# Threshold attention and a bilinear FFN on one core: another order inside the first ten slots

## The chip, the cores and the metric

The kernel runs on one core of one Trainium2 chip, as one launch. The time is device microseconds (us) of that core. The core has a matrix engine (TensorE, "PE" in the profile, with its weight loads as "PEld"), a vector engine (VectorE, "DVE"), an activation engine (ScalarE, "ACT"), a general engine (GpSimd, "POOL") and a queue that issues the transfers (SyncE, "SP"). Each works through its own list of instructions in the order in which the program wrote it, and waits on semaphores of the others.

## The reference

```python
# q, k, v: (8, 8, 576, 64) float32, tau = 0.02; w_a, w_b: (512, 1536), w_out: (1536, 512), float64
scores = 1/sqrt(64) * q @ k^T
thresh = max(scores, -1) - tau
scores = where(scores >= thresh, scores, -1e9)
scores = scores - max(scores, -1)
attn   = exp(scores); attn = attn / (sum(attn, -1) + 1e-9)
x      = (attn @ v) with the heads beside each other        # (4608, 512)
out    = ((x @ w_a) * (x @ w_b)) @ w_out                    # (4608, 512) float32
```

The weights of the FFN arrive as float64 and are made float32 on the chip, by operations on their two 32-bit halves.

## The kernel before

**Units and slots.** Attention is cut into 160 units. A unit is 128 rows of the queries of two heads (a pair), or the last 64 rows of both. The loop at line 756 runs over slots: slot g computes the scores of unit g, its exponentials, mask and sums, and carries units g-1 and g-2 (in the first ten slots) further. After the loop the rest of the FFN follows. The order in which the program writes the instructions is kept on every engine (`keep_order`), so where a call stands in the loop is where its instructions stand in each engine's list.

**What one of the first slots does**, for the unit of slot g, in the order of before:

- `scores` (line 314): 16 records of products on TensorE, two row maxima on VectorE (L332), two biases (L334) and one threshold (L336) on GpSimd.
- `weighted_unit` (line 499), in slots 2 to 9, for unit g-2: `product` (L479, TensorE, product with v), then `join`: a copy out of PSUM on ScalarE (L468) and an addition of the other half on VectorE (L469); then `exchange`, two copies on GpSimd (L489).
- `convert_sign` and `convert_shift` (L238, L246, VectorE) and `convert_add` (L251, GpSimd) for the weight pieces that slot g-1 began.
- `load_weights`: transfers of the next weight pieces on SP's queue, when a staging buffer is free, which the sign operation frees.
- `weigh` (line 353): two exponentials on ScalarE (L364), then two operations on VectorE that mask and sum (L367).
- `turn_pe` (line 396), in slots 1 to 8, for unit g-1: 16 records of products that turn and scale the weights (L406, TensorE), two copies on ScalarE (L408), 4 records more (L412), one copy on VectorE (L414).
- `convert_first` (L225, L226, ScalarE) and `convert_clamp` (L232, GpSimd) of one piece, then `reciprocal` (L376, L380), `diagonals` (L393, ScalarE; from unit 8 on `normalise`, L386), then the slot's other pieces. Slots 0 to 3 begin two pieces, slots 4 to 9 three.
- `advance`: steps of the FFN on TensorE. The amount is counted in columns: a slot has a `pace`, and `advance` runs steps until the columns owed are paid. A step of the first block has 128 columns (8 records of L578 in the trace). In slots 0 to 8 the whole pace, 0.04 x 36864 + 576 = 2051 columns, comes at the end of the slot, and 640 columns are taken off for `product`. If there is no block to work on, what is owed is dropped. The first block exists from slot 5 on, when the product of unit 3 is joined.

One step in eight ends a group of products: after the eighth with `wa_sb` ScalarE copies the result out (L584), after the eighth with `wb_sb` VectorE multiplies (L586). Until then the group holds its PSUM buffer.

**PSUM.** All results of TensorE go through one pool of four buffers (`banks`, two banks each). A unit's two score buffers are held from the products to the mask operations, which read them again.

**Slots from 10 on** differ: the turning is done by VectorE transposes and transfers, and the FFN's columns come in four portions over the slot.

Of the kernel before, what the change touches and what calls it, by code (L numbers as in the profile page):

```python
# [10 lines left out]
FP32 = mybir.dt.float32  # L11
# [12 lines left out]
BY_PE = 8  # L24
# [8 lines left out]
PORTIONS = (0.3, 0.35, 0.15, 0.2)  # L33
RAWS = 4
BY_HEAD = 16


def keep_order(tc):
# [13 lines left out]
def kernel(  # L52
# [40 lines left out]
    P = 128  # L93
# [21 lines left out]
    def pool(name, bufs, **kw):  # L115
        return ctx.enter_context(tc.tile_pool(name=name, bufs=bufs, **kw))
# [4 lines left out]
    small = pool("small", 2)  # L121
# [3 lines left out]
    def banks(n, name):  # L125

        return psum.tile([P, 2, 512], FP32, tag="banks", name=name)[:, :, 0:n]
# [4 lines left out]
    loaded = {}  # L132
# [110 lines left out]
    def convert_shift(n):  # L243
        if n in stages:
            top = pieces[n][0].bitcast(U32)
            nc.vector.tensor_scalar(top, top, 3, None, op0=ALU.logical_shift_left)  # L246
# [43 lines left out]
    prepared, scored, weights, turned, tbufs = {}, {}, {}, {}, {}  # L290
# [23 lines left out]
    def scores(i, u):  # L314
# [3 lines left out]
        each = [(c, t, j) for c in range(2) for t in range(n) for j in range(2)]  # L318
        if units.index((i, u)) < BY_HEAD:
            each.sort(key=lambda x: x[2])  # L320
# [29 lines left out]
        t = t.rearrange("p n e -> p (n e)").rearrange("p (z n e) -> p z n e", z=4, e=Q)  # L350
        return [t[:, i]] if u == NT else [t[:, g % 2 * 2 + j] for j in range(2)]

    def weigh(i, u):

        sc, thr, bias, mx, biased = scored.pop((i, u))
        n = len(sc)
        sums = small.tile([P, 2], FP32, tag="sums", name="sums")
        ws = rooms_of(i, u)
        sb = [s.rearrange("p c (n e) -> p c n e", e=Q) for s in sc]
        wb = [w.rearrange("p (c n) e -> p c n e", c=2) for w in ws]  # L360
        for j in range(n):
            if not biased:
                nc.scalar.activation(bias[:, j:j + 1], mx[:, j:j + 1], AF.Copy, scale=e_nscale)
            nc.scalar.activation(wb[j], sb[j], AF.Exp, bias=bias[:, j:j + 1], scale=e_scale)  # L364
        for j in range(n):
            wv = wb[j]
            nc.vector.scalar_tensor_tensor(  # L367
                out=wv, in0=sb[j], scalar=thr[:, j:j + 1], in1=wv,
                op0=ALU.is_ge, op1=ALU.mult, accum_out=sums[:, j:j + 1])
        weights[i, u] = (ws, sums)  # L370
# [25 lines left out]
    def turn_pe(i, u):  # L396

        ws, dg = weights.pop((i, u))
        ws = [w.rearrange("p n e -> p (n e)") for w in ws]
        wT = work.tile([P, NSLOT, P], FP32, tag="wT", bufs=WT_BUFS, name="wT")  # L400
        turned[i, u, "pe"] = wT
        tp = banks(512, "tp").rearrange("p j (s q) -> p j s q", s=NT)
        for j, w in enumerate(ws):
            for s in range(NT):
                c = TAIL * j + s * P
                nc.tensor.matmul(tp[:, j, s, :], w[:, c:c + P], dg[:, j], start=True, stop=True)  # L406
        for j in range(2):
            nc.scalar.copy(wT[:, 5 * j:5 * j + NT], tp[:, j])  # L408
        tp = banks(P, "tp")[:, 0]
        for j, w in enumerate(ws):  # L410
            c = MAIN * (1 - j)
            nc.tensor.matmul(tp[TAIL * j:TAIL * (j + 1)], w[:, c:c + TAIL], dg[:, j],  # L412
                             start=True, stop=True)
        nc.vector.tensor_copy(wT[:, NT], tp)  # L414
# [56 lines left out]
    def product(wT, vm, n):  # L471

        pv = banks(n, "pv")
        for s in (NT, 0, 1, 2, 3):
            for r in range(2):
                rows = slice(r * D, (r + 1) * D)
                for j in ((r,) if s == NT else range(2)):
                    k0 = NT if s == NT else 5 * j + s
                    nc.tensor.matmul(pv[j * D:(j + 1) * D, r], vm[rows, k0], wT[rows, k0],  # L479
                                     start=(s == (NT if j == r else 0)), stop=(s == NT - 1))  # L480
        return pv

    def x_tile(name):
        return work.tile([P, HP, HALF], FP32, tag="xT", bufs=XT_BUFS, name=name)
# [11 lines left out]
                exchange(x, xs, hp, 0, HALF, nc.gpsimd)  # L496
            blocks.append(((x, xs), what))

    def weighted_unit(i, u):

        b, hp = pairs[i]
        pv = product(turned.pop((i, u, "pe")), loaded[i]["v"], P)
        if (b, 0) not in x_of:
            x_of[b, 0] = x_tile("xT")
            state["xs"] = x_tile("xS")
        join(x_of[b, 0][:, hp, u * P:(u + 1) * P], pv[:, 0], pv[:, 1])
        exchange(x_of[b, 0], state["xs"], hp, u * P, (u + 1) * P, nc.gpsimd)
        if hp == HP - 1:
            state["rows"] = u + 1
            if u == 0:  # L510
                blocks.append(((x_of[b, 0], state["xs"]), ("first", b, 0)))
# [181 lines left out]
    def cost():  # L693

        return BLOCK_COLS - (NF // 2 * CH if state["sums"] else 0)
# [34 lines left out]
    def backlog():  # L730
        return len(blocks) * cost() + (running["left"] if running["ffn"] is not None else 0)
# [3 lines left out]
    units = []  # L735
# [15 lines left out]
    n = 0  # L751
# [4 lines left out]
    for g in range(len(units) + PV_LAG):  # L756
        written = len(pending)
        here = g < len(units)
        converting = bool(early.get(g)) or bool(early.get(g - 1))
        if here:  # L760
            i, u = units[g]
            scores(i, u)
        turn_back()
        exchange_blocks()
        pace = (PACE if g > BY_PE else PACE_EARLY) * BLOCK_COLS
        if g > BY_PE:
            pace = min(pace, backlog() / (min([a for a in arrivals if a > g] + [len(units) + PV_LAG + 1]) - g))
        pace += (NSLOT + 1) // 2 * S / (NT + 1) + CATCH_UP * max(backlog() - BLOCK_COLS, 0)
        if 2 <= g < BY_PE + 2:
            weighted_unit(*units[g - 2])  # L770
            running["owed"] -= (NSLOT + 1) // 2 * P
        if g < 3:
            prep_copy(*prep_pe(g + 1, "q"))
        for n in early.get(g - 1, []):
            convert_sign(n)
        for n in early.get(g - 1, []):
            convert_shift(n)
        for n in early.get(g - 1, [])[-1:] + early.get(g - 1, [])[:-1]:
            convert_add(n)
        if g == 3:  # L780
            for c in range(0, NSUM - 2 * CW + 1, 2 * CW):
                extra.append(sums_u32[:, c:c + 2 * CW].rearrange("p (f w) -> p f w", w=2))
        load_weights(RAWS)
        if g > BY_PE and g <= len(units):
            turn_blocks(*units[g - 1])
        if g > BY_PE:
            advance(PORTIONS[0] * pace)
        if here:
            weigh(i, u)
        if 0 < g <= BY_PE:  # L790
            turn_pe(*units[g - 1])
        if g < 3:
            prep_copy(*prep_pe(g + 1, "k"))
        for p in range(HP, NPR):
            for name, d in (("q", 2), ("k", 1)):
                if g == first[p] - d:
                    prep(p, name)
        if g > BY_PE:
            advance(PORTIONS[1] * pace)
            n = g - PV_LAG  # L800
            if BY_PE <= n < len(units) and part(*units[n]):
                make_room()
                weighted(*part(*units[n]))
                running["owed"] -= (NSLOT + 1) // 2 * width(*part(*units[n]))
        for n in early.get(g, [])[:1]:
            convert_first(n)
            convert_clamp(n)
        if here:
            reciprocal(i, u, nc.scalar if converting else nc.vector)
        if here and g < BY_PE:  # L810
            diagonals(i, u)
        elif here:
            normalise(i, u)
        for n in early.get(g, [])[1:]:
            convert_first(n)
            convert_clamp(n)
        load_weights(RAWS)
        for p in range(HP, NPR):
            for name, d in (("q", 4), ("k", 3)):
                if g == first[p] - d:  # L820
                    load(p, name)
        for p in range(1, NPR):
            if g == first[p] - 1:
                load_v(p)
        store(written)
        advance((PORTIONS[2] if g > BY_PE else sum(PORTIONS[:3])) * pace)
        advance(PORTIONS[3] * pace)

        if not converting and not state["sums"]:
            state["slots"] = state.get("slots", 0) + 1  # L830
            for n in {1: (0,), 2: (1,), 3: (2,)}.get(state["slots"], ()):
                for z in range(2):
                    weight_sums(n, z)
            if state["slots"] >= 3 and state["through"]:
                for z in range(2):
                    weight_sums(3, z)
                state["sums"] = True
# [38 lines left out]
```

## Time and profile before

| | |
|---|---|
| median of 8 runs | 1480.96 us (1477.71 to 1483.95) |
| the profiled execution: its time, its span | 1478.24 us, 1476.4 us |
| busy, share of the span | PE 96%, PEld 82%, DVE 63%, ACT 45%, POOL 24% |
| mean granted TensorE clock | 0.994 |
| chain that ended last, by engine | PE 86%, DVE 5%, ACT 2%, the rest 7% |
| start of the scores of slots 2 to 10 | 25.86, 33.97, 39.48, 46.37, 56.47, 67.47, 76.53, 87.68, 101.0 us |

The time of an execution is its span and 1.84 us around it. The span runs from the first to the last instruction; all places in the trace are us from its start. Busy time of TensorE is modelled, since its products overlap. An engine's idle time matters only where it lies on the way to the end.

### The profile page before, as it was taken

The numbers are of one execution on the slowest core, as the hardware profiler recorded it, in microseconds if no ns is written. First come the engines' busy times: TensorE is split into PE (matmuls) and PEld (weight loads), VectorE is DVE, ScalarE is ACT, GpSimd is POOL, SyncE is SP. The second block draws the span as 40 slices with busy tenths as digits, with TensorE's granted clock in tenths as the row PEclk, the third lists the DMA queues.
The fourth block names the chain that finished last, engine by engine and source line by source line (L and its number), as shares of the span: only waits on it lengthen the run. The fifth ranks groups of instructions, "written<-read, shape, count | busy, mean of one in ns | idle before, by whom it ended". The sixth has DMA issues, their size and how long they took to land.

```text
span 1476.4 us, 57127 instructions
## 1 busy us (share of the span) xinstructions
PE 1419.5 (96%) x25344; PEld 1211.1 (82%) x25344; DVE 926.2 (63%) x2068; ACT 669.6 (45%) x1213; POOL 359.9 (24%) x563
## 2 busy tenths in 40 slices
PE   5678999999999999999999999999999999999998
PEld 4566587898779898897888999889888888888886
DVE  5767678778666775775646766576656766623212
ACT  4866355555544554554434544355444554411010
POOL 3876512203030312032222213120404040310000
PEclk9999999999999999999999999999999999999999
DMA  9956898889867976796647876588757977530000
GB/s 206 215 168 169 171 175 185 196 158 186 209 150 152 194 182 135 176 184 162 138 105 140 182 167 149 117 186 186 162 133 140 188 174 163 134 90 16 2 17 16
DMA packets 624582, 220.75 MB, mean 150 GB/s; under 512 B 542928, under 2 KB 612048, under 8 KB 624336
## 3 DMA queue, kind: packets, MB, share of 16 engines
q1 hardware_dynamic: 621968, 216.52, 67.0%
q8 instruction: 199, 3.26, 0.9%
q10 hardware_dynamic: 2368, 0.59, 0.2%
q14 instruction: 47, 0.39, 0.1%
HBM read 127.40 MB, written 89.65 MB: 147 GB/s over the span
## 4 chain that ended last, share of the span: by engine, by line
PE 86%; DVE 5%; ACT 2%; SPq 2%; DMA 2%; issue 1%; POOL 1%; ACTq 0%; DVEq 0%; POOLq 0%
PE pab L578 47%; PE po L621 19%; PE pv L479 9%; PE sc L325 9%; PE po L665 1%; DVE mx L332 1%; DVE low L238 1%; DVE tw L433 1%; DVE tw L367 1%; ACT tw L364 1%; SPq L143 1%; SPq L151 0%; SPq L441 0%; SPq L206 0%; DMA swap<-tw 0%
## 5 line engine op out<-in xcount | busy, mean ns | idle before, releaser
L332 DVE TENSOR_REDUCE mx<-sc 128x1 f32<-128x576 f32 x288 | 205.1, 749 | 128.1 <-PE sc L325 117.3
L578 PE MATMUL pab<-xS,wa_sb 64*64 64x256 f32 (+1 forms) x3584 | 271.2, 370 | 0.9 <-POOL xS L489 0.9
L578 PE MATMUL pab<-xS,wb_sb 64*64 64x256 f32 (+1 forms) x3584 | 268.1, 372 | 0.0
L325 PE MATMUL sc<-kT,qT 64*64 64x288 f32 x2304 | 241.1, 408 | 20.6 <-DVE kT L312 7.9
L590 POOL TENSOR_TENSOR h<-h 128x256 f32<-128x256 f32 x168 | 117.3, 730 | 542.2 <-PE po L621 539.1
L578 PE MATMUL pab<-xT,wb_sb 64*64 64x256 f32 (+1 forms) x3200 | 236.7, 370 | 5.6 <-DVE h L586 4.1
L578 PE MATMUL pab<-xT,wa_sb 64*64 64x256 f32 (+1 forms) x3200 | 236.8, 368 | 5.3 <-POOL thr L336 2.1
L621 PE MATMUL po<-wo_sb,h 64*64 64x256 f32 x3264 | 241.1, 376 | 0.0
L386 ACT ACTIVATE tw<-tw,rcp 128x576 f32<-128x576 f32 x244 | 176.1, 768 | 130.1 <-DVE rcp L380 130.0
L364 ACT ACTIVATE tw<-sc,bias,scalars 128x576 f32<-128x576 f32 x260 | 214.6, 831 | 38.6 <-POOL bias L334 25.4
L578 PEld LDWEIGHTS pab<-xS,wa_sb 64*64 64x64 f32 x3584 | 193.7, 133 | 29.6 <-POOL xS L489 5.2
L367 DVE SCALAR_TENSOR_TENSOR tw<-sc,thr,tw 128x576 f32<-128x576 f32 x260 | 203.6, 802 | 21.2 <-ACT tw L364 20.0
L578 PEld LDWEIGHTS pab<-xS,wb_sb 64*64 64x64 f32 x3584 | 196.1, 134 | 23.2 <-issue 0.2
L621 PEld LDWEIGHTS po<-wo_sb,h 64*64 64x64 f32 x3264 | 178.0, 132 | 23.6
L578 PEld LDWEIGHTS pab<-xT,wa_sb 64*64 64x64 f32 x3200 | 171.6, 133 | 28.4 <-DVE kept L469 4.3
L578 PEld LDWEIGHTS pab<-xT,wb_sb 64*64 64x64 f32 x3200 | 172.4, 134 | 26.2 <-DVE h L586 4.5
L479 PE MATMUL pv<-wT,vm 64*64 64x320 f32 (+3 forms) x2592 | 186.1, 379 | 5.0 <-ACT h L584 3.2
L325 PEld LDWEIGHTS sc<-kT,qT 64*64 64x64 f32 x2304 | 144.7, 133 | 50.5 <-issue 14.2
L621 PE MATMUL po<-sums_u,h 64*64 64x256 f32 x2448 | 181.1, 376 | 0.0
L433 DVE STREAM_TRANSPOSE tw<-tw 128x576 f32<-128x576 f32 x240 | 171.6, 753 | 0.2 <-ACT tw L386 0.2
L586 DVE TENSOR_TENSOR h<-h,pab 128x512 f32<-128x512 f32 (+1 forms) x112 | 73.4, 655 | 149.0 <-PE pab L578 141.2
L479 PEld LDWEIGHTS pv<-wT,vm 64*64 64x64 f32 x2592 | 142.7, 134 | 25.6 <-ACT h L584 4.2
(85 smaller groups left out, 1236.7 us busy)
## 6 DMA issues: line engine op xcount, KB each, us to landing
swap<-tw SPq DMA_DIRECT2D x240, 288.0 KB, 5.3
wT<-swap SPq DMA_DIRECT2D x28, 1440.0 KB, 7.5
wT<-swap SPq DMA_DIRECT2D x32, 1152.0 KB, 6.4
vm<-in_v_dram SPq DMA_DIRECT2D x32, 288.0 KB, 4.7
qT<-in_q_dram SPq DMA_DIRECT2D x112, 72.0 KB, 3.6
kT<-in_k_dram SPq DMA_DIRECT2D x112, 72.0 KB, 5.0
swap<-wt SPq DMA_DIRECT2D x112, 72.0 KB, 2.8
out_dram<-kept SPq DMA_DIRECT2D x30, 256.0 KB, 4.2
```

The source lines that it names most:

```text
L143: engine.dma_start(t[r], rows[:, :, h * Q:(h + 1) * Q])
L325: nc.tensor.matmul(sc[j if u < NT else 0][to, c], qT[r, q0:q0 + D], kT[r, c * SH:(c + 1) * SH], start=True, stop=True)
L332: nc.vector.tensor_reduce(mx[:, c], sc[j], axis=AX.XY, op=ALU.max)
L364: nc.scalar.activation(wb[j], sb[j], AF.Exp, bias=bias[:, j:j + 1], scale=e_scale)
L367: nc.vector.scalar_tensor_tensor(out=wv, in0=sb[j], scalar=thr[:, j:j + 1], in1=wv, op0=ALU.is_ge, op1=ALU.mult, accum_out=sums[:, j:j + 1])
L386: nc.scalar.activation(w, w, AF.Copy, scale=rcp[:, j:j + 1])
L433: nc.vector.transpose(w, w)
L479: nc.tensor.matmul(pv[j * D:(j + 1) * D, r], vm[rows, k0], wT[rows, k0], start=(s == (NT if j == r else 0)), stop=(s == NT - 1))
L578: nc.tensor.matmul(pab[c * D:(c + 1) * D, r], w[rows, f // n, k, fs + c * D:fs + (c + 1) * D], moving, start=(k == 0), stop=(k == H - 1))
L586: nc.vector.tensor_tensor(ht, ht, pab, op=ALU.mult)
L590: (nc.vector if state["over"] else nc.gpsimd).tensor_tensor(*a, **kw)
L621: nc.tensor.matmul(po[c * D:(c + 1) * D, r, y], ht[rows, t0:t0 + D], other[rows, f], start=(f == 0), stop=(f == NF // 2 - 1))
```

## The change

`weigh` is split into `exponentials` and `masks`. In slots 0 to 9 the exponentials stand ahead of the join of the product with v, and both stand behind the sign and shift operations; `weighted_unit` becomes the product, in its old place, and `join_unit`, behind the exponentials. In slots 0 to 8 the FFN's columns come in four parts: 0.4 of the pace between the scores and the product, 0.2 behind the turning, and 0.2 and 0.2 at the end of the slot. From slot 10 on the code is the same; in slot 9 the portions of the FFN are the same.

```diff
@@ -33,6 +33,7 @@
 PORTIONS = (0.3, 0.35, 0.15, 0.2)
 RAWS = 4
 BY_HEAD = 16
+EARLY = (0.4, 0.2, 0.2)
 
 
 def keep_order(tc):
@@ -350,11 +351,10 @@
         t = t.rearrange("p n e -> p (n e)").rearrange("p (z n e) -> p z n e", z=4, e=Q)
         return [t[:, i]] if u == NT else [t[:, g % 2 * 2 + j] for j in range(2)]
 
-    def weigh(i, u):
+    def exponentials(i, u):
 
         sc, thr, bias, mx, biased = scored.pop((i, u))
         n = len(sc)
-        sums = small.tile([P, 2], FP32, tag="sums", name="sums")
         ws = rooms_of(i, u)
         sb = [s.rearrange("p c (n e) -> p c n e", e=Q) for s in sc]
         wb = [w.rearrange("p (c n) e -> p c n e", c=2) for w in ws]
@@ -362,6 +362,12 @@
             if not biased:
                 nc.scalar.activation(bias[:, j:j + 1], mx[:, j:j + 1], AF.Copy, scale=e_nscale)
             nc.scalar.activation(wb[j], sb[j], AF.Exp, bias=bias[:, j:j + 1], scale=e_scale)
+        weights[i, u] = ws, sb, wb, thr
+
+    def masks(i, u):
+        ws, sb, wb, thr = weights[i, u]
+        n = len(ws)
+        sums = small.tile([P, 2], FP32, tag="sums", name="sums")
         for j in range(n):
             wv = wb[j]
             nc.vector.scalar_tensor_tensor(
@@ -496,10 +502,9 @@
                 exchange(x, xs, hp, 0, HALF, nc.gpsimd)
             blocks.append(((x, xs), what))
 
-    def weighted_unit(i, u):
+    def join_unit(i, u, pv):
 
         b, hp = pairs[i]
-        pv = product(turned.pop((i, u, "pe")), loaded[i]["v"], P)
         if (b, 0) not in x_of:
             x_of[b, 0] = x_tile("xT")
             state["xs"] = x_tile("xS")
@@ -766,8 +771,11 @@
         if g > BY_PE:
             pace = min(pace, backlog() / (min([a for a in arrivals if a > g] + [len(units) + PV_LAG + 1]) - g))
         pace += (NSLOT + 1) // 2 * S / (NT + 1) + CATCH_UP * max(backlog() - BLOCK_COLS, 0)
+        if g <= BY_PE:
+            advance(EARLY[0] * pace)
         if 2 <= g < BY_PE + 2:
-            weighted_unit(*units[g - 2])
+            i2, u2 = units[g - 2]
+            pv = product(turned.pop((i2, u2, "pe")), loaded[i2]["v"], P)
             running["owed"] -= (NSLOT + 1) // 2 * P
         if g < 3:
             prep_copy(*prep_pe(g + 1, "q"))
@@ -775,6 +783,10 @@
             convert_sign(n)
         for n in early.get(g - 1, []):
             convert_shift(n)
+        if g < BY_PE + 2:
+            exponentials(i, u)
+        if 2 <= g < BY_PE + 2:
+            join_unit(i2, u2, pv)
         for n in early.get(g - 1, [])[-1:] + early.get(g - 1, [])[:-1]:
             convert_add(n)
         if g == 3:
@@ -786,9 +798,12 @@
         if g > BY_PE:
             advance(PORTIONS[0] * pace)
         if here:
-            weigh(i, u)
+            if g >= BY_PE + 2:
+                exponentials(i, u)
+            masks(i, u)
         if 0 < g <= BY_PE:
             turn_pe(*units[g - 1])
+            advance(EARLY[1] * pace)
         if g < 3:
             prep_copy(*prep_pe(g + 1, "k"))
         for p in range(HP, NPR):
@@ -823,7 +838,7 @@
             if g == first[p] - 1:
                 load_v(p)
         store(written)
-        advance((PORTIONS[2] if g > BY_PE else sum(PORTIONS[:3])) * pace)
+        advance((PORTIONS[2] if g > BY_PE else EARLY[2]) * pace)
         advance(PORTIONS[3] * pace)
 
         if not converting and not state["sums"]:
```

## The prediction

> **What bounds the kernel now.** I read the busy time by stretches first, then the waits of the first hundred us, then the order of time inside one slot. The columns of the first view are stretch, its length, then busy us and instructions of PE, PEld, DVE, ACT and POOL, then clock, DMA share and GB/s.
>
> ```profile
> 0.00:101.00 101.00, 67.44 (x1185) 56.02 (x1187) 65.61 (x152) 65.73 (x129) 64.93 (x99) 0.97 0.89 197
> 101.00:165.00 64.00, 54.49 (x1056) 43.17 (x1052) 48.28 (x101) 38.19 (x66) 42.56 (x51) 0.97 0.70 172
> 165.00:300.00 135.00, 133.77 (x2338) 106.47 (x2334) 98.72 (x223) 69.64 (x123) 30.43 (x47) 0.99 0.83 179
> ```
>
> From 165 us on PE is busy 133.77 of 135.00 us: there only its work counts, and the change leaves that as it is. Ahead of it PE stands idle 33.6 us in slots 0 to 9 (up to 101 us) and 9.5 us in the next 64. So the change is worth what it does to the length of slots 0 to 9, passed on almost whole, plus or minus what the next slots give back. In the first 101 us PE, DVE, ACT and POOL are all busy about two thirds: no engine is the bound, a ring of waits is. The waits between 33.9 and 101 us (engine, line waited for, us, times, longest):
>
> ```profile
> DVE xT L469 <- ACT xT L468: 7.0, 5, 1.9
> ACT xT L468 <- PE pv L479: 6.2, 5, 2.4
> ACT wT L408 <- PE tp L406: 3.2, 4, 1.1
> PE pv L479 <- ACT h L584: 3.2, 2, 1.6
> PE tp L406 <- DVE xT L469: 2.1, 3, 0.7
> ```
>
> The first line is what the change goes for: DVE waits for the copy of the join, with signs and shifts behind it that wait for nothing. The last line matters as much: the turning waits for the join's addition. It reads nothing of the join; what it waits for is the PSUM buffer of `product`. With two score buffers held until the masks and one by an open group of the FFN, the fourth goes from `product` to the turning. One slot (6) in the order of time:
>
> ```profile
> 60.11 0.54 POOL L334 TENSOR_SCALAR bias<-mx,scalars 128x1 f32<-128x1 f32 x2
> 60.74 0.27 ACT L468 COPY xT<-pv 128x128 f32<-128x128 f32 x1 [1.44 <-PE pv L479]
> 60.90 1.56 ACT L364 ACTIVATE tw<-sc,bias,scalars 128x576 f32<-128x576 f32 x2
> 61.04 0.29 DVE L469 TENSOR_TENSOR xT<-xT,pv 128x128 f32<-128x128 f32 x1 [1.94 <-ACT xT L468]
> 61.38 2.05 PE L406 MATMUL tp<-dg,tw 128*128 128x128 f32 x16 [0.72 <-DVE xT L469]
> 63.52 1.07 ACT L408 COPY wT<-tp 128x512 f32<-128x512 f32 x2 [1.06 <-PE tp L406]
> 66.27 0.69 ACT L393 ACTIVATE dg<-ident,rcp 128x128 f32<-128x128 f32 x2 [0.23 <-DVE rcp L380]
> 70.28 0.83 ACT L364 ACTIVATE tw<-sc,bias,scalars 128x576 f32<-128x576 f32 x1 [0.21 <-POOL bias L334]
> ```
>
> The reader is to see that the exponentials (60.90 to 62.46) run while PE turns (61.38 to 63.43): they hide the turning from ACT, whose copies wait only 1.06 us for it. The next exponentials start at 70.28, so this ring took 9.38 us. Slots 7, 8 and 9 begin theirs at 70.28, 81.11 and 92.02: three rings in 31.12 us, 10.37 each.
>
> **The change part by part.**
>
> *Slots 0 to 2: 0 us.* Without a join (slots 0, 1) each engine's list is the same. In slot 2 the addition moves behind signs and shifts, but the masks stand behind all of them in both orders, and the next scores wait for the key copy on DVE (wait 33.17 to 33.9) as before.
>
> *FFN parts.* Without a block the owed columns are dropped, so the parts do something from slot 5 on. In slot 5 before, 2051-640 columns give 12 steps (96 records at 53.83 to 56.4, as seen). After, the 820 of the first part come ahead of the join that makes the block and are lost: 1230-640 columns, 5 steps. In slots 6, 7 and 8 it is 11 steps either way: before all at the end, after 7 between scores and product (820 columns), none behind the turning (the 640 are paid there), 1 and 3 at the end. A step takes 0.215 us (11 in 65.02 to 67.36), so 1.5 us of PE work moves in front of `product`, into a time when PE waits (1.65 us in slot 6); that is cover, and it costs nothing. The 7 steps that slot 5 loses are 1.5 us of PE to be done later. The pace of slots 9 to 19 divides the backlog by the slots to the next arrival, so they are made up there, where PE has 9.5 us idle up to 165 us. Between 0 (all in idle time) and +1.5 I take the middle: **+0.75 us**.
>
> *Exponentials ahead of the join, slots 6 to 8.* Moved behind two exponentials on ACT: one copy of 0.27. Moved behind three signs and three shifts on DVE (2.08 and about 1.0): one addition of 0.29. Behind that addition are queued the masks on DVE, the two exchange copies and three additions on POOL, and, by the buffer, the turning. After slot 6's, 7's and 8's first part, 12, 23 and 34 steps are done, 4, 7 and 2 into a group of eight: a group is open each time, so the turning has no other buffer and starts after the join, and that after the exponentials. New ring from exponentials to exponentials: exponentials 1.56; copy and addition started 0.04+0.30 (60.74 to 61.04) later; addition to turning 0.34 (61.04 to 61.38): 2.20 with rounding of starts, where it was 0.48 (60.90 to 61.38). From the turning to the next exponentials the order is as before: 8.90 (61.38 to 70.28). Sum 11.10. Up to 0.6 comes off, because POOL's additions no longer wait until 64.48 for the shifts and the third piece's clamp may end at 69.4 instead of 69.98. And something is added, seen in slot 10, where signs already follow the maxima directly:
>
> ```profile
> 103.04 0.29 POOL L334 TENSOR_SCALAR bias<-mx,scalars 128x1 f32<-128x1 f32 x1
> 103.52 1.89 DVE L238 SCALAR_TENSOR_TENSOR low<-raw,low 128x512 uint32<-128x512 uint32 x3
> 103.70 1.17 POOL L334 TENSOR_SCALAR bias<-mx,scalars 128x1 f32<-128x1 f32 x1 [0.38 <-DVE mx L332]
> 104.90 0.83 ACT L364 ACTIVATE tw<-sc,bias,scalars 128x576 f32<-128x576 f32 x1 [0.24 <-POOL bias L334]
> ```
>
> A bias beside a sign took 1.17 us, the one ahead of it 0.29. Over slots 2 to 9 the bias of before has a median of 0.285 us, over slots 10 to 15 (signs right behind the maxima) 0.826 us with up to 1.536, and ACT waited 6.8 us for biases there, 1.3 before. The changed order puts slots 3 to 9 into that state: +0.54 on the first bias by the medians, between 0 and 1.2. Ring: 11.10-0.6+0.54 = 11.0, bounds 10.5 and 11.6. Three rings: 33.0 against 31.12, **+1.9 us** (+0.4 to +3.7).
>
> The Trainium skill has the rule behind that row (page "SBUF — State Buffer", section "Who interferes with whom"): a VectorE instruction with two SBUF inputs and a GpSimd one that reads SBUF exclude each other, the later blocked for the whole instruction of the other. By it a bias would wait at most one sign (0.69 here) each time; the row's 0.88 is more than one sign. With 0.69 in place of 0.54 the three rings would be 0.45 us longer; the measured medians decide here.
>
> *Slots 3 to 5.* In slot 3 the second bias (36.72) falls beside signs; the masks, at 38.72 before, come 0.3 to 0.6 late, and with them the buffers of slot 4's scores. In slot 4 the bias comes late from the clamps (43.01) and again meets signs. In slot 5 there is no open group yet and DVE gains: it waited 1.86 us for the copy at 50.93. Bounds -0.5 and +1.5 at slot 6's exponentials; I take **+0.5 us**.
>
> *Slot 8's multiplication.* Step 32, the fifth of slot 8's first part, ends a group with `wb_sb`: its multiplication (L586) now stands between maxima and signs on DVE, and needs ACT's copy of the other half (ended at step 24, in slot 7), which stands behind slot 7's conversions. In slot 8 before, such a copy came at 78.23, with DVE idle 3.28 us ahead of the multiplication, which had 1.4 us of maxima split around it. Queued behind it now: signs, shifts, join, masks. Bounds 0 and +2.0; **+1.4 us**, since maxima end about 2 us ahead of that copy in the sum above.
>
> *Slot 9.* ACT waited 2.57 us for the masks there (sums at 98.61) behind DVE's multiplication and transposes, so a late ACT is partly absorbed: 0 to -1.7, taken **-0.8 us**.
>
> *Transfers.* The loads on SP waited 46.0 us for signs (DVE L238) up to 165 us; the signs now come no later relative to the maxima, and the DMA engines are busy throughout up to 75 us. Nothing gained, nothing lost: 0.
>
> Sum: 0.75+1.9+0.5+1.4-0.8 = **+3.75 us**. The profiled execution took 1478.24 us (span 1476.4 and 1.84 around it), which is 2.72 below the median 1480.96; on the median the forecast is 1484.7 us. The sum of the low bounds is -1.8, of the high ones +8.7: 1479.2 to 1489.7.
>
> **The rivals.**
>
> *Faster: the turning finds a buffer.* If `product` and the turning get different buffers (the allocation is not in the profile), the turning hides under the exponentials again, ring: 1.56+0.31+1.07 and 5.8 from the first conversion (64.48) to 70.28 = 8.75, near POOL's own chain. Then 3 x (10.37-8.8) = 4.7 and some 1.3 in slot 9: -6, 1475 us. For it: all four engines have a third of their time free, and PE's end of a slot is 7 steps shorter. Against it: the three waits of L406 for L469, and the count of open groups.
>
> *No change.* Bias collisions are short and slots 10 to 16 absorb the rest: low bounds of rings and multiplication, +0.5, 1481.5 us. For it the 9.5 us of idle PE up to 165 us.
>
> *Much slower: slot 9's bias.* If the third clamp of slot 8 is as late as ACT's conversions (3.6 us by the same sums), bias and exponentials of slot 9 come after its signs, and transposes and masks follow late instead of absorbing. It decides as soon as the exponentials end after the shifts: 0.5+1.9+1.4+3.6+1.5 = +9, 1490 us.
>
> **How the numbers follow.** About 0.2% (3 us) is what a measurement of this kernel can tell from no change. Forecast 0.48, of it 0.40 slower by more than that and 0.08 within; faster rival 0.27 (0.25 and 0.02 within); no change 0.16; much slower 0.09. That makes faster 0.25, same 0.26, slower 0.49. The range reaches from below the faster rival's time, 1473, to 1491, which leaves out the tails beyond both.
>
> **What would show it.** Right: starts of slots 7 to 10 later by 1 to 4 us; exponential rings of 10.5 to 11.6; bias near 0.8 us in slots 3 to 9; ACT waiting about 2 us for the turning; DVE no longer waiting for the join's copy but for L584 in slot 8; 40 records of L578 in slot 5. Wrong: L406 not waiting for L469, rings under 10, or slots 10 to 16 swallowing or multiplying the difference.

## The result, and the profile after

The changed kernel takes 1491.3 us in the median of 11 runs (1489.29 to 1500.14), the kernel before 1480.94 us in the median of 32: ratio 1.0081, 95% interval 1.0068 to 1.0095. It is 10.4 us slower by the medians, where 3.75 was forecast. The profiled execution has a span of 1492.8 us and a time of 1494.61, 3.3 above its median. The profiled execution of before lies 2.7 below its own, so the two profiles are 16.4 us apart where the medians are 10.4 apart; places in the trace below are of these two executions.

The busy time by stretches, with the columns of the prediction:

```profile
0.00:101.00 101.00, 66.77 (x973) 55.69 (x975) 61.34 (x136) 56.67 (x113) 58.69 (x88) 0.92 0.85 182
101.00:165.00 64.00, 50.60 (x1119) 43.67 (x1111) 47.43 (x99) 41.84 (x73) 42.94 (x54) 0.89 0.62 159
165.00:300.00 135.00, 132.08 (x2196) 103.47 (x2196) 94.04 (x210) 64.61 (x114) 38.24 (x55) 0.99 0.83 178
```

In the first 101 us every engine did less than before (PE 973 records for 1185, ACT 113 for 129), while the granted clock fell from 0.97 to 0.92, and in the next stretch from 0.97 to 0.89. Most of the loss is there by slot 10. The starts in the order of time show where:

| | before | after | late by |
|---|---|---|---|
| scores of slot 2 | 25.86 | 26.82 | 0.96 |
| exponentials of slot 6 | 60.90 | 66.66 | 5.76 |
| exponentials of slot 7 | 70.28 | 80.17 | 9.89 |
| exponentials of slot 8 | 81.11 | 92.04 | 10.93 |
| exponentials of slot 9 | 92.02 | 105.21 | 13.19 |
| scores of slot 10 | 101.0 | 113.91 | 12.91 |
| end of the span | 1476.4 | 1492.8 | 16.4 |

The waits between 33 and 114 us of the kernel after (in its line numbers: L364 exponentials, L335 bias, L412 turning, L414 its copies, L474 and L475 join, L583 FFN, L589 its copy):

```profile
ACT wT L414 <- PE tp L412: 13.7, 4, 4.3
ACT tw L364 <- POOL bias L335: 12.3, 8, 3.0
PE tp L412 <- DVE xT L475: 9.2, 3, 3.8
DVE xT L475 <- ACT xT L474: 8.2, 6, 1.8
PE pab L583 <- ACT h L589: 5.9, 1, 5.9
```

VectorE still waits for the join's copy (8.2 us, 7.0 before), although signs and shifts now fill the time ahead of it. ScalarE waits for biases, which it hardly did. The turning waits up to 3.8 us where 0.7 was the longest. Slot 6 in the order of time:

```profile
63.88 1.04 POOL L233 TENSOR_SCALAR wa_sb<-wa_sb 128x512 f32<-128x512 f32 x1
65.93 1.12 POOL L335 TENSOR_SCALAR bias<-mx,scalars 128x1 f32<-128x1 f32 x2
66.66 1.55 ACT L364 ACTIVATE tw<-sc,bias,scalars 128x576 f32<-128x576 f32 x2 [3.01 <-POOL bias L335]
68.11 0.26 ACT L474 COPY xT<-pv 128x128 f32<-128x128 f32 x1
68.40 0.29 DVE L475 TENSOR_TENSOR xT<-xT,pv 128x128 f32<-128x128 f32 x1 [1.49 <-ACT xT L474]
68.74 3.79 PE L412 MATMUL tp<-dg,tw 128*128 128x128 f32 x16 [3.73 <-DVE xT L475]
72.62 1.07 ACT L414 COPY wT<-tp 128x512 f32<-128x512 f32 x2 [4.25 <-PE tp L412]
80.17 1.55 ACT L364 ACTIVATE tw<-sc,bias,scalars 128x576 f32<-128x576 f32 x2 [1.93 <-POOL bias L335]
```

The reader is to see three things. The clamp of 63.88 took 1.04 us and not 0.61: it too stands beside signs now, and the bias behind it comes late. The exponentials no longer cover the turning, so ScalarE idles 4.25 us. And the turning took 3.79 us, not 2.05: after 3.73 us of waiting PE ran it at a lower clock (0.57 granted between 70 and 75 us, 1.00 there before).

### The profile page after: what moved, and what is told of

Same layout as the page of the kernel before. It is cut to its first block, busy times and chain, and to the rows that moved or that the text cites. A ratio compares the mean times of both kernels' runs of the same rounds, so it can differ in the third digit from the quotient of the medians.

```text
span 1492.8 us, 57123 instructions
## 1 busy us (share of the span) xinstructions
PE 1430.3 (96%) x25344; PEld 1206.9 (81%) x25344; DVE 929.4 (62%) x2068; ACT 669.0 (45%) x1213; POOL 361.8 (24%) x563
## 4 chain that ended last, share of the span: by engine, by line
PE 86%; DVE 4%; DMA 3%; ACT 2%; POOL 2%; issue 2%; SPq 1%; ACTq 0%; DVEq 0%; POOLq 0%
PE pab L583 46%; PE po L626 18%; PE sc L326 10%; PE pv L485 9%; DMA swap<-tw 2%; PE po L670 1%; DVE mx L333 1%; PE tp L412 1%; SPq L447 1%; DVE tw L439 1%; ACT tw L364 1%; POOL bias L335 1%; DVE tw L373 1%; POOL wa_sb L252 0%; DMA scalars<-in_tau_dram 0%
## 5 line engine op out<-in xcount | busy, mean ns | idle before, releaser
L583 PE MATMUL pab<-xS,wa_sb 64*64 64x256 f32 (+1 forms) x3584 | 273.4, 371 | 0.9 <-POOL xS L495 0.9
L583 PE MATMUL pab<-xS,wb_sb 64*64 64x256 f32 (+1 forms) x3584 | 269.8, 374 | 0.1
L583 PE MATMUL pab<-xT,wb_sb 64*64 64x256 f32 (+1 forms) x3200 | 238.3, 371 | 10.7 <-ACT h L589 5.9
L583 PE MATMUL pab<-xT,wa_sb 64*64 64x256 f32 (+1 forms) x3200 | 238.1, 371 | 4.3 <-DVE kept L475 2.1
L364 ACT ACTIVATE tw<-sc,bias,scalars 128x576 f32<-128x576 f32 x260 | 214.7, 831 | 53.6 <-POOL bias L335 37.2
L583 PEld LDWEIGHTS pab<-xS,wa_sb 64*64 64x64 f32 x3584 | 192.5, 133 | 32.0 <-POOL xS L495 5.3
L583 PEld LDWEIGHTS pab<-xS,wb_sb 64*64 64x64 f32 x3584 | 195.1, 135 | 25.5 <-issue 0.9
L583 PEld LDWEIGHTS pab<-xT,wb_sb 64*64 64x64 f32 x3200 | 171.8, 134 | 33.4 <-ACT h L589 6.1
L583 PEld LDWEIGHTS pab<-xT,wa_sb 64*64 64x64 f32 x3200 | 170.1, 134 | 30.2 <-DVE kept L475 4.3
```

Source lines behind the costliest of these rows:

```text
L583: nc.tensor.matmul(pab[c * D:(c + 1) * D, r], w[rows, f // n, k, fs + c * D:fs + (c + 1) * D], moving, start=(k == 0), stop=(k == H - 1))
```

## The experiments

Three theories stood at the start. A: biases (and what else GpSimd does) blocked beside the signs. B: the turning waits for the PSUM buffer of a join that now stands behind the exponentials. C: the FFN part ahead of the product. Later came K: the clock that falls in a long wait is what makes B dear. All ratios are to the kernel before, with 95% intervals; 0.1% is 1.5 us.

| | FFN at the end | FFN parts moved | no FFN in slots 0 to 8 |
|---|---|---|---|
| old order | 1 | 0.9968 | 0.9987 |
| exponentials ahead of the join | 1.0092 | | 1.0079 |
| signs and shifts ahead of the join | 1.0046 | | |
| both | 1.0098 | 1.0081 (the change) | 1.0047 |
| both, biases on VectorE | | 1.0041 | 0.9993 |
| old order, biases on VectorE | | 0.9989 | |

**The parts one by one.** Where nothing else is said, the diffs are against the changed kernel; `...` marks lines left out, and the conditions on `g` around `join_unit` are left out too.

`e1_parts`, the FFN parts alone:

```diff
         pv = product(...)
+        join_unit(i2, u2, pv)
         ... signs, shifts
-        if g < BY_PE + 2:
-            exponentials(i, u)
-        join_unit(i2, u2, pv)
...
         if here:
-            if g >= BY_PE + 2:
-                exponentials(i, u)
+            exponentials(i, u)
             masks(i, u)
```

> Only the FFN parts are moved (0.4 of the pace between scores and product, 0.2 behind the turning); exponentials, signs, shifts and join stay in their old order. Theory A (biases blocked on GpSimd beside signs) and theory B (the turning waits for the PSUM buffer of the join): within 1.5 us of the kernel before, since neither a bias nor the join moves. Theory C (the FFN part ahead of the product is what costs, by holding a PSUM buffer and putting copies in front of the exponentials): most of the 10.4 us, over +6.

Measured: 1475.0 us, ratio 0.9968 (0.9954 to 0.9983). Theory C falls, and A and B were wrong in expecting no change here: the parts are not neutral, they gain 0.32%.

`e2_exp`, the exponentials alone:

```diff
-        if g <= BY_PE:
-            advance(EARLY[0] * pace)
         pv = product(...)
+        exponentials(i, u)
+        join_unit(i2, u2, pv)
         ... signs, shifts
-        exponentials(i, u)
-        join_unit(i2, u2, pv)
... the other two advance calls as before the change
```

> Only the exponentials are put ahead of the join; signs and shifts stay behind the join, the FFN at the end of the slot. Theory A: the bias has no sign beside it, so its median stays at 0.29 us and the time rises by 0 to 3 us. Theory B: the turning still waits for the exponentials by way of the join, its wait for L475's addition grows to 2 to 4 us per slot, the clock falls in those slots, and the time rises by 6 to 10 us. Theory C: no change.

Measured: 1493.74 us, ratio 1.0092 (1.0075 to 1.0109), dearer than the whole change. No sign stands beside a bias here, so A is not all there is.

`e3_signs`, signs and shifts alone:

```diff
-        if g <= BY_PE:
-            advance(EARLY[0] * pace)
         pv = product(...)
         ... signs, shifts
-        exponentials(i, u)
         join_unit(i2, u2, pv)
...
+            exponentials(i, u)        # in every slot ahead of masks, as before
             masks(i, u)
... the other two advance calls as before the change
```

> Only signs and shifts are put ahead of the join (and so beside the biases); the join's copy stays ahead of the exponentials on ScalarE, the FFN at the end of the slot. Theory A: bias median 0.7 us, ScalarE waits some 10 us for biases in slots 2 to 9, the time rises by 5 to 9 us. Theory B: the join waits for the signs on VectorE but no longer for the exponentials, so the turning waits about 1.5 us instead of 0.7 per slot: +1 to +4 us. Theory C: no change.

Measured: 1486.01 us, ratio 1.0046 (1.0032 to 1.0060), +6.8 us. The size is A's, but ScalarE waited only 4.4 us for biases between 33 and 112 us, and the turning 8.5 us for the join (longest 3.4): B's wait, behind signs in place of exponentials.

`e4_noparts`, both without the parts (the `advance` calls as before the change):

> The changed kernel without its FFN parts (all of a slot's FFN at its end, as before). If the parts gain in the new order what they gained in the old one (4.7 us): +13 to +17 us over the kernel before. If their gain belongs to the old order alone: +8 to +12 us.

Measured: 1493.68 us, ratio 1.0098 (1.0081 to 1.0115), +14.5 us. The parts gain 0.17% in the new order and 0.32% in the old; the intervals don't tell these two apart.

**Theory A.** `e5_bias`, the changed kernel with the biases on the engine that has the maxima:

```diff
-                nc.gpsimd.tensor_scalar(bias[:, c], mx[:, c], e_nscale, ...)
+                (nc.vector if units.index((i, u)) < BY_PE + 2 else nc.gpsimd).tensor_scalar(bias[:, c], ...)
```

> The changed kernel, with the two biases of slots 0 to 9 computed on VectorE (0.15 us each, ahead of the signs) in place of GpSimd; all else as changed. Theory A: the exponentials start about 0.3 us after the maxima, and most of the 10.4 us comes back: 0 to +3 us over the kernel before. Theory B: the join is still behind two exponentials and the turning behind it, so it comes back only by the earlier start of the exponentials: +4 to +8 us over the kernel before. Theory C: little comes back, +8 us or more.

Measured: 1485.75 us, ratio 1.0041 (1.0027 to 1.0056). Half of the 0.81% comes back: blocked biases are about half of the loss. A wait that is left, between 60 and 112 us of this run, and the turnings of slots 6 and 7 behind it:

```profile
PE tp L412 <- DVE xT L475: 7.3, 3, 3.2
64.53 3.47 PE L412 MATMUL tp<-dg,tw 128*128 128x128 f32 x16 [2.43 <-DVE xT L475]
76.28 2.46 PE L412 MATMUL tp<-dg,tw 128*128 128x128 f32 x16 [3.24 <-DVE xT L475]
```

`c1_parts_bias` puts the same line into the kernel of `e1_parts`:

> The kernel before with only the FFN parts moved, and the biases of slots 0 to 9 on VectorE instead of GpSimd: what the runs so far point to as better than both. Theory A: biases no longer stand behind GpSimd's clamps, ScalarE waits less for them: 4 to 8 us faster than the kernel before. Theory B: the biases were not what the turning waited for in that order, so about as fast as the parts alone, 3 to 6 us faster than the kernel before.

Measured: 1480.13 us, ratio 0.9989 (0.9975 to 1.0002). In the old order the biases on VectorE gain nothing, rather lose 0.2% against the parts alone: most were not blocked there (median 0.284 us in slots 3 to 9 of e1_parts). So e5_bias still stands 0.52% behind its partner in the old order.

**Theory B.** Four kernels without any FFN in slots 0 to 8, so that no open group holds a buffer (the diff is against the kernel before):

```diff
-        advance((PORTIONS[2] if g > BY_PE else sum(PORTIONS[:3])) * pace)
-        advance(PORTIONS[3] * pace)
+        if g > BY_PE:
+            advance(PORTIONS[2] * pace)
+            advance(PORTIONS[3] * pace)
+        else:
+            running["owed"] = 0.0
```

`n_before`, in the old order:

> The old order with no FFN in slots 0 to 8: the partner of n_after. All theories: slower than the kernel before, by up to the 45 steps of 0.215 us that are put off (9.7 us), less what later slots take into idle time; 2 to 9 us.

Measured: 1478.5 us, ratio 0.9987 (0.9972 to 1.0001). Putting off 45 steps costs nothing; the prediction had already priced seven of them at 0.75 us. But more of its biases were blocked beside signs than in the kernel before, although the order is the same: their median in slots 3 to 9 is 0.736 us for 0.285, and ScalarE waited 6.0 us for them.

`n_after`, in the new order:

> The new order of exponentials, signs, shifts and join, with no FFN at all in slots 0 to 8 (its work is done later), to be compared with n_before, the old order with the same FFN. No group of the FFN is open at the turning, so a fourth PSUM buffer is free for it. Theory B (the open group leaves the turning only the buffer of the join): the difference between the two falls from some +15 us (without the parts) to +0 to +5 us. Theory A (blocked biases) and any theory that does without the buffer: it stays at +8 us or more.

Measured: 1487.74 us, ratio 1.0047 (1.0030 to 1.0065), 0.60% over its partner where it was 0.98% with FFN. So what needs the FFN is a part of the cost, and the rest stayed. In the order of time, slot 6 of n_after:

```profile
61.14 2.05 PE L411 MATMUL tp<-dg,tw 128*128 128x128 f32 x16
66.07 0.96 POOL L334 TENSOR_SCALAR bias<-mx,scalars 128x1 f32<-128x1 f32 x2
66.80 1.55 ACT L363 ACTIVATE tw<-sc,bias,scalars 128x576 f32<-128x576 f32 x2 [3.55 <-POOL bias L334]
```

The turning starts without a wait and takes 2.05 us, long before the exponentials; what is left is ScalarE waiting 3.55 us for a bias (20.2 us in nine times between 33 and 112 us). The turning's four last records (L417) still waited for the join's addition, 18.9 us in six times: with two score buffers, the product's and the turning's first part, the four are taken. No engine is shown waiting for these records.

`n_after_bias` takes the wait for the biases away too, by the line of e5_bias:

> The new order of exponentials, signs, shifts and join, no FFN in slots 0 to 8 (as n_after, which is +9.2 us over n_before), and the biases of slots 0 to 9 on VectorE. Theories A and B together (blocked biases and the buffer are all there is): 0 to +3 us over n_before. If a third thing costs: +5 us or more.

Measured: 1478.69 us, ratio 0.9993 (0.9981 to 1.0004), 0.06% over n_before: nothing that can be told from zero. Without blocked biases and without FFN in slots 0 to 8 the cost of the new order is gone, though L417 still waited 12.8 us. Two things stay open. n_before pays for blocked biases itself, and the old order with neither was not run, so that the new order is no faster than the old one is not shown. And leaving out the FFN takes away its copies and multiplications with its buffer; that the buffer is what counts rests on the turning, which no longer waits in the trace.

`n_exp`, the exponentials alone ahead of the join, without FFN:

> Only the exponentials ahead of the join, signs and shifts behind it, and no FFN in slots 0 to 8; partner n_before (measured 0.9987 of the kernel before). No sign stands beside a bias and no group is open at the turning. Theory B (the 14 us of the exponentials alone come from the turning's wait for the join's buffer): they fall to 0 to +4 us over n_before, and L411 no longer waits for the join's addition. If the exponentials cost by something else, as by the later join itself: +8 us or more.

Measured: 1491.37 us, ratio 1.0079 (1.0067 to 1.0091). B as stated fails for this order: no group, no blocked bias (median 0.292 us in slots 3 to 9), and still 0.92% over n_before. Its waits between 33 and 112 us:

```profile
DVE xT L474 <- ACT xT L473: 25.2, 7, 4.7
ACT sums L381 <- DVE tw L372: 17.4, 7, 4.8
```

VectorE waits for the join, with up to three signs, three shifts and the masks behind it; ScalarE then waits for the masks (in n_before the two waits are 10.5 and 4.7 us). Read so, the join behind the exponentials is dear by what is queued behind the join; no run tests this alone. In the change the signs stand ahead of the join, and in n_after VectorE's wait is 10.1 us, which fits that both together without FFN (1.0047) cost less than the exponentials alone.

**Theory K.** `e6_warm`, the changed kernel with the product repeated:

```diff
-        for s in (NT, 0, 1, 2, 3):
+        for s in (NT, 0, 1, 2, 3) * times:       # times = 3 in slots 5 to 8
```

> The changed kernel with the product with v computed three times in slots 5 to 8 (the first two results are overwritten by the third): 2.6 us of needless TensorE work per slot, in the time in which TensorE waits for the join. Theory K (the long wait lets the granted clock fall, and the turning and what follows then run at half speed): the waits in front of L412 shrink, the turning takes about 2.05 us in slots 6 and 7 instead of 3.79, and the kernel is 2 to 6 us faster than the changed one, that is +4 to +8 us over the kernel before. Theory B alone (the order of the waits, whatever the clock): 0 to +3 us over the changed kernel, +10 to +13 over the one before.

Measured: 1497.55 us, ratio 1.0114 (1.0092 to 1.0136). The turnings of slots 5 to 8 did take 2.05 us each, and the kernel was slower all the same. But the repeated product itself ran late, and ScalarE's copy of the join then waited for it (8.0 us in two waits), so the price of the clock can't be read from it.

`f_fill`, filler behind the product instead:

```diff
+        if 6 <= g <= BY_PE:
+            fill(10)      # 10 x 4 products of ident by ident into unused columns of the open group's buffer
```

> The changed kernel with filler work for TensorE between the product with v and the turning, in slots 6 to 8: 40 small products (10 steps' worth, about 2.2 us at full clock) into unused columns of the open FFN group's own PSUM buffer, read by nobody. Unlike the tripled product it does not delay the join. Theory K (the wait of 3.7 to 3.8 us ahead of the turning lets the granted clock fall, and the turning then takes 3.79 us): the longest wait falls under 2 us, the turning takes 2.05 us, and the kernel with more work is 2 to 6 us faster than the changed one (+4 to +8 us over the kernel before). If the clock does not matter: 0 to +2 us over the changed kernel.

Measured: 1492.06 us, ratio 1.0076 (1.0053 to 1.0098), as the change. The turnings of slots 6 and 7 of this run:

```profile
71.97 3.52 PE L413 MATMUL tp<-dg,tw 128*128 128x128 f32 x16
85.09 3.60 PE L413 MATMUL tp<-dg,tw 128*128 128x128 f32 x16 [2.38 <-DVE xT L476]
```

The waits are gone or shorter, but the turnings were nearly as slow as without filler. In slot 6 the granted clock was 1.00 up to 71 us, while three quarters of the filler ran and in the 1.80 us of idle time behind them, and 0.50 from 72 to 75 us, when the turning ran. So the filler did not test what the fallen clock costs.

`f_fill_bias`, filler and biases on VectorE:

> The same filler, and the biases of slots 0 to 9 on VectorE: the changed order with both the blocked biases and the fallen clock taken away, the open group still there. If the buffer costs by the clock that falls: +0 to +3 us over the kernel before (the biases alone gave +6.05). If it costs by the order of the waits itself: +5 us or more.

Measured: 1487.41 us, ratio 1.0053 (1.0033 to 1.0072), not told apart from e5_bias (1.0041). Here only slot 6's turning was slow (2.86), slots 7 and 8 took 2.05, and the time did not come down. But from slot 6's exponentials to slot 7's it took 16.07 us, for 12.95 in e5_bias, so the filler has a price of its own. The share of the slow turnings is better read from e5_bias: from slot 6's exponentials to slot 9's it took 35.72 us, 29.14 in c1_parts_bias, and its two slow turnings make up 1.42 and 0.41 of these 6.58 us. The turnings themselves are the smaller part of B's price there.

**Where the parts gain.** `l_lag`, slot 5 short by seven steps, nothing else (against the kernel before):

```diff
-        advance((... else sum(PORTIONS[:3])) * pace)
+        advance((... else sum(PORTIONS[:3]) - 0.4 * (g == 5)) * pace)
```

> The kernel before, with all its FFN at the end of the slots, but slot 5 runs 5 steps of it and not 12, as in the kernel with the parts moved. If the 4.7 us that the parts gain come from the seven steps that slot 5 loses (and from where groups begin and end in later slots): 3 to 6 us faster than the kernel before. If they come from the steps placed ahead of the product: within 1.5 us of the kernel before.

Measured: 1477.54 us, ratio 0.9986 (0.9975 to 0.9997), between the two expectations.

`p_full5`, the parts with slot 5's twelve steps (against e1_parts):

```diff
-        advance(PORTIONS[3] * pace)
+        advance((PORTIONS[3] + 0.4 * (g == 5)) * pace)
```

> Only the FFN parts are moved, as in the run that was 4.7 us faster than the kernel before, but slot 5 gets back the 0.4 of its pace that is dropped there, and so runs 12 steps as before. If the gain comes from the steps placed ahead of the product in slots 6 to 8: 3 to 6 us faster than the kernel before. If it comes from slot 5's missing steps: within 2 us of it.

Measured: 1478.27 us, ratio 0.9974 (0.9961 to 0.9988): most of the parts' gain is there without the missing steps, though the interval reaches into that of l_lag.

`c3_all_ahead`, `EARLY = (0.8, 0.0, 0.0)` in the kernel of e1_parts:

> Only the FFN parts are moved, with 0.8 of the pace ahead of the product in place of 0.4, 0.2 and 0.2: fewer steps between the turning and the next scores. If that stretch of TensorE is what the parts shorten: 5 to 8 us faster than the kernel before. If the ring lies elsewhere: no better than the parts as they were (3 to 6 us).

Measured: 1478.95 us, ratio 0.9988 (0.9974 to 1.0003). A larger dose gains no more than the smaller one, so the gain is not simply the steps taken out of the stretch between turning and scores; slot 5 loses all its twelve steps here. One difference in the profiles is where a group ends. In slot 9 of the kernel before, PE waited for a multiplication that stood behind signs and transposes; in e1_parts two shorter waits stand in its place (first line before, the others e1_parts):

```profile
97.15 1.98 PE L578 MATMUL pab<-xT,wb_sb 64*64 64x128 f32 x32 [2.68 <-DVE h L586]
```

```profile
91.80 1.10 PE L583 MATMUL pab<-xT,wb_sb 64*64 64x128 f32 x32 [1.82 <-DVE xT L475]
96.81 1.10 PE L583 MATMUL pab<-xT,wb_sb 64*64 64x128 f32 x32 [1.28 <-DVE tw L373]
```

From slot 9's scores to slot 10's it took 10.48 us for 13.32, but slot 10 gave all of that back (13.54 for 8.67). So slot 9 is not shown to be where the parts gain. That they gain is shown; how is not settled.

**Which kernel to keep.** `e1_parts` is the fastest measured, 0.32% ahead of the kernel before and 1.1% ahead of the changed one.

## Why the prediction was right or wrong

**Direction and causes: right.** Slower, by the two waits named: L412 for the join's addition by way of the buffer, and biases beside signs. e5_bias, n_after and n_after_bias show both, each with about half: 0.40% for the biases with FFN and 0.54% without it; and for what needs the FFN, 0.52% between e5_bias and c1_parts_bias. The bias median in slots 2 to 9 went from 0.285 to 0.686 us (said: near 0.8).

**Rings of slots 6 to 8: a failing term.** Said 11.0 each, 33.0; measured 13.51, 11.87 and 13.17, 38.55. The ring from slot 6 splits into 2.08 up to the turning (said 2.20), 3.88 from there to its copies (2.14 in the row used) and 7.55 on to the next exponentials (6.76 in the row; the sum took off 0.6 and put on 0.54). So 1.74 us in each of the first two rings is the turning's own duration, taken from a row in which PE had waited 0.72 us; these 3.5 us are most of what the three rings have over 34.4, that is 33.0 and the 1.4 for slot 8's multiplication. The last ring had no slow turning (2.05 us). The Trainium skill has the rule that was passed over (page "TensorE: Matmul & The Clock Gate", section "Part 1: The HAM clock gate"): after an idle window of some 3.4 us the clock goes to half. This row agrees, with a wait of 3.73 us, a granted clock of 0.57 and a duration of 1.85 times the old one; but a wait of 2.43 us in e5_bias was enough for 3.47 us. In the change's own time the share of the clock was not isolated.

**Slots 3 to 5: the other failing term.** Said +0.5, at most +1.5, at slot 6's exponentials; measured +5.76. Of this, 1.40 was there at slot 3's exponentials (37.89 for 36.49) and lies inside the spread of executions: up to there six kernels with the old order run the same instructions, and theirs start anywhere from 36.35 to 40.46 us. From there to slot 6's exponentials it took 28.77 us for 24.41, and this is no matter of one execution: 24.03 to 25.34 in those six kernels, 27.68 to 29.07 in the five with the change's order and the biases on GpSimd, 21.95 to 22.49 in the three with that order and the biases on VectorE; the old order with that line, c1_parts_bias, took 24.22. So blocked biases cost some 6 us in these three slots, and without them the order would have gained about 2. The sum had priced only the bias itself. GpSimd's clamps stand beside signs as well, and both biases come behind them, one after the other, in the same stretch. Slot 4:

```profile
44.64 1.05 POOL L233 TENSOR_SCALAR wb_sb<-wb_sb 128x512 f32<-128x512 f32 x1
45.67 1.38 POOL L335 TENSOR_SCALAR bias<-mx,scalars 128x1 f32<-128x1 f32 x2
46.97 1.55 ACT L364 ACTIVATE tw<-sc,bias,scalars 128x576 f32<-128x576 f32 x2 [2.30 <-POOL bias L335]
```

The clamp took 1.05 us for 0.61, and ScalarE waited 2.30, 2.16 and 3.01 us for the biases of slots 4 to 6.

**Slot 8's multiplication: right.** Maxima ended at 90.78, signs began at 92.23, behind the multiplication that waited for ScalarE's copy: 1.45 us for the 1.4 said.

**Slot 9: sign right, size too large.** It was to give back 0.8 us; 13.19 us late at its exponentials, 12.91 at slot 10's scores, it gave back 0.28. Behind the exponentials stood ScalarE's copy of an FFN group, for which PE waited 5.86 us. The condition of the rival "much slower" held: the biases of slot 9 came beside its last sign, took 1.68 us for two, and ScalarE waited 1.47 us. But that the measured +10.4 is near its +9 is luck. Of that +9, 5.1 were to come from slot 9's late clamp and what follows it; measured, 10.93 of the 13.19 us stood there already at slot 8's exponentials, and the ring from slot 8, 13.17, is only 0.8 over the 11.0 and 1.4 of the sum.

**The FFN parts: wrong sign.** Said +0.75 us, between 0 and 1.5; measured -0.32% in the old order. In the new one it is -0.17%, which the intervals don't tell from zero. n_before shows that steps put off are free here; by what the parts gain stays open.

**The faster rival.** With a free buffer the turning's 16 records were hidden again, as it said, but n_after pays at the biases. With those gone too, n_after_bias is 0.06% over its partner and 0.07% under the kernel before, not 6 us under it. Its rings from slots 6 and 7 took 8.82 and 8.91 us, near the 8.75 of the rival; but the three rings of n_before are short as well, 25.72 us for its 27.31.

## What to carry to other kernels

Before an operation is moved into an idle gap of one engine, list which instructions of the other engines then stand beside it and which buffers stay held: here signs in VectorE's gap slowed the clamps and biases of GpSimd beside them, and a later join held the buffer that the turning needed. Price a new wait of TensorE together with the speed of what follows it, not by a row of an undisturbed slot. And run the parts of a change alone: one of three here was a gain of 0.32% that the other two buried.

## What the runs showed of the hardware

- GpSimd instructions beside a run of VectorE's bitwise operations take longer: a bias of 0.29 us became 1.17 beside signs of 0.69, so it was held for longer than one sign lasts, and clamps of 0.61 became 1.05. The signs pay too: three took 2.80 us at 62.67, beside clamps, for 2.08 before.
- A turning of 16 records took 2.05 us at full clock and 3.79 after 3.73 us of waiting; it also took 3.47 in e5_bias after a wait of only 2.43 us, and 3.52 to 3.60 in f_fill behind filler work, most of which had run at a granted clock of 1.00. Work shortly before did not keep the clock up there.
